# Reordering the hand-over from retention to the first expert: one weight load, one row load, the memsets and one index computation

## The chip, the cores and the metric

The kernel runs on one core of a Trainium2 chip. The metric is the device time of one execution in microseconds; the time before is the median of three runs. Two runs of this kernel differ by less than 0.2%.

## The reference, cut to what matters

```
# retention, per batch b and head h: B, H, S, D = 4, 8, 768, 64
state = gamma[h] * state + outer(k[t], v[t])
y[t]  = scale * q[t] @ state
# x: the 3072 tokens of all batches, 512 features each (8 heads x 64)
logits = x @ w_gate                       # 8 experts
e      = argmax(logits);  g = softmax(logits)[e]
out[t] = g * (relu(x[t] @ w1[e]) @ w2[e]) # w1[e]: 512 x 1024, w2[e]: 1024 x 512
```

Every token goes to exactly one expert. All arithmetic is float32; the kernel gets float32 products on TensorE from three products of a high and a low part each (hi·hi, lo·hi, hi·lo).

## The kernel before, in words

**Retention (L498 to L581).** The 24 chunks of 128 tokens are handled two at a time, in 12 passes `k` of one loop. A pass makes the scores of both chunks (`scores`, L253: TensorE L259, masked on VectorE L262), carries the state in (`carry`, L280: TensorE L289), multiplies the scores with the values (`output`, L293: TensorE L300) and turns the result into `xT` on VectorE (`turn_out`, L303, L308). It also makes the logits of the two chunks of the pass before (`logits` L328, `rows` L312, `finish_logits` L335). The order on every engine is the order in which the code is written (`manual_schedule`).

**Gating and sending.** The chunks fall into six groups (L55). For each group `choose`, `soft`, `rank`, `slots`, `weights` and `advance` (L360 to L433) find the expert of each token, its slot in that expert's region of a DRAM buffer `xs_dram`, its weight (L429) and its token number (L430), and `send_x` (L319) scatters the chunk's rows there with one indirect DMA, whose descriptors GpSimd makes (L719, about 1 us each). Behind the counted rows of an expert 96 rows are set to zero (`clear`, L325, and `clear_rows`, L713), so that a padded load reads zeros.

**Weights.** Each expert has four quarters of 1 MB (`fetch`, L135: parts 0 and 1 are w1, 2 and 3 are w2). SyncE issues these loads; they go into two buffers `raw` in turn. `split` (L142) makes the high part on ScalarE (L147) and the low part on VectorE (L148). So a quarter can be loaded only when the quarter two before it has been split in full. Expert 0's 16 split pieces lie in the passes of the loop (table `SPLITS`, L59): pieces 10 and 11, the last two of w2's first half, in pass 10. `fetch(1, 0)` (L639) therefore waits for piece 11.

**The hand-over (L583 to L679).** Expert 0 has two sets of rows. The first 192 (`xg0`, region 8) are loaded in pass 9 and computed from pass 11 on (`early_half`, L747: TensorE L761 and L779), which fills TensorE while the last groups are gated and sent. The others, `xg1`, up to 224 late rows of region 8's neighbour `E`, come only after the last chunk has been sent. SyncE's order there is: `fetch(1, 0)`, the clearing of expert 1's tail (L640), `xg1` (L641), expert 1's rows `xgs[:, 1]` (L642), three small loads of token numbers and weights into `meta0` (L643 to L645), `fetch(1, 1)` (L646), then 12 register loads (L637, L638). VectorE turns `xg1` (L729), ScalarE rounds it to the high part (L738), VectorE makes the low part (L739), and `token_index` (L194, L199 to L207) makes the scatter indices of all late rows from `meta0` (L679).

**The experts (`moe_main`, L793).** For each expert 8 blocks `f` of the first layer (TensorE L947, into PSUM tiles `phs` in turn, three of them) and then `steps` products of the second layer (L989 for experts 0 and 7, L991 for the others). After each block ScalarE makes the high part `hh` (L959) and VectorE the low part `hl` (L961). What else an engine does is put behind a block by the table `jobs` (L912): splits of the next expert's weights, loads, scatters. For expert 0 the order on VectorE behind the blocks is: `hl` of each, the splits of quarter (1, 0) behind blocks 2 and 3, of (1, 1) behind 5 and 6. Then, at the second layer, four turns of expert 1's rows (L729; three of their low parts are made by GpSimd, L739), two splits of (1, 2), and the weighted result rows (`put_rows`, L876, VectorE L882) of the two products.

**Two details.** The third product of expert 0's second layer (rows beyond 192, rarely any) stands under a branch on TensorE, with nothing on the other side (L996):

```
if e == 0 and k == 2:
    with tc.If(fewer[0] > 0):
        second_layer(cap)
```

And `moe_main` begins with four memsets of PSUM tiles on VectorE (`rare` L815, the three `phs` from column 392 on, L817) and one of `zero` on GpSimd (L825), which the scheduler puts in between the hand-over's instructions. Expert 1 and the later ones write only the columns that their token count needs (`by_count`, L834: 392 of 440 for expert 1 here), while ScalarE and VectorE read all 440. The framework orders all accesses to a bank of PSUM within a tile, whichever columns they touch.

Of the kernel before, what the change touches and what calls it, by code (L numbers as in the profile page):

```python
# [9 lines left out]
F32 = mybir.dt.float32  # L10
# [45 lines left out]
CHOSEN = {3: 0, 6: 1, 9: 2, 10: 3, 11: 4}  # L56

SENDS = {4: (0, 1), 5: (1, 3), 6: (3, 5), 7: (5, 7), 8: (7, 10), 9: (10, 12), 10: (12, 16), 11: (16, 20)}
SPLITS = {4: (0, 1), 5: (2, 3), 7: (4, 5), 8: (6, 7), 9: (8, 9), 10: (10, 11)}  # L59
FETCHES = {1: 0, 4: 1, 6: 2, 9: 3}  # L60


# [50 lines left out]
def retention_moe(ctx, tc, qkv, wts, cst, gdec, out):  # L113
# [95 lines left out]
    with ExitStack() as actx:  # L209
# [102 lines left out]
        def rows(g):  # L312
            xp = ps_s.tile([P, DM], F32, name="xp", tag="sp")
            for p in range(NP):
                nc.tensor.transpose(out=xp[:, p * P:(p + 1) * P], identity=ident,
                                    in_=xTs[g // 2][:, p, (g % 2) * C:(g % 2 + 1) * C])
            nc.scalar.copy(out=xn(g)[:, :, 0:C], in_=xp.rearrange("a (q m) -> a q m", q=4))
# [10 lines left out]
        def logits(t):  # L328
            L = ps_m.tile([P, TW], F32, name="L", tag="mm")
            for p in range(NP):  # L330
                nc.tensor.matmul(out=L[32 * p:32 * p + 32, :], lhsT=wgs[:, p, :], rhs=xTs[t][:, p, :],
                                 start=True, stop=True)
            nc.scalar.copy(out=LT, in_=L)

        def finish_logits(t):  # L335
            k = max(i for i, (a, n) in enumerate(GROUPS) if a <= 2 * t)
            first, n = GROUPS[k]
            late = int(first >= NCH // 2)
            lp = ps_m.tile([P, 2, NP, 32], F32, name="lp", tag="mm")
            for ci in range(2):  # L340
                nc.tensor.transpose(out=lp[:, ci].rearrange("t p e -> t (p e)"),  # L341
                                    in_=LT[:, ci * C:(ci + 1) * C], identity=ident)
            at = 2 * t - first
            if at == 0:
                lgs[k] = gsm.tile([P, CPB, E], F32, name="lg", bufs=2)[:, 0:n]
            nc.vector.tensor_reduce(out=lgs[k][:, at:at + 2, :], axis=AX.X, op=ALU.add,
                                    in_=lp[:, :, :, late:late + E].rearrange("t c p e -> t c e p"))

        def gating(k):
# [73 lines left out]
            def weights():  # L423
                gw = sm("gw")
                nc.vector.tensor_reduce(out=gw, in_=v["ex"], axis=AX.X, op=ALU.add)
                nc.vector.tensor_scalar(out=gw, in0=gw, scalar1=1e-9, scalar2=None, op0=ALU.add)
                a = first % (2 * CPB)
                rows = ring[:, a:a + n]
                nc.vector.reciprocal(out=rows[:, :, :, C + 1], in_=gw.broadcast_to([P, n, 4]))  # L429
                nc.vector.scalar_tensor_tensor(  # L430
                    out=rows[:, :, :, C].bitcast(I32), scalar=4.0, op0=ALU.mult, op1=ALU.add,
                    in0=k_("tok")[:, gn].unsqueeze(2).broadcast_to([P, n, 4]),
                    in1=k_("row").unsqueeze(1).broadcast_to([P, n, 4]))  # L433

            return dict(choose=choose, soft=soft, rank=rank, slots=slots, advance=advance, weights=weights)

        def fill(n):
            for i in range(state["half"], state["half"] + n):
# [145 lines left out]
        stages["rank"](ps_s, "sp")  # L584
        for name in ("slots", "weights", "advance"):
            stages[name]()
        logits(NCH // 2 - 1)
        rows(NCH - 2)
        rows(NCH - 1)
        finish_logits(NCH // 2 - 1)  # L590
        for g in range(SENDS[NCH // 2 - 1][1], GROUPS[-1][0]):
            send_x(g)
# [1 line left out]
        final["choose"]()  # L594
        final["soft"]()
        fill(FILL[1])
        lows(1, nc.gpsimd)
        final["rank"](ps_s, "sp")
        fill(FILL[2])
        final["slots"]()  # L600
# [36 lines left out]
        number = lambda i: nc.sync.value_load(eid7[0:1, i - 1:i], min_val=1, max_val=E - 1)  # L637
        end_of = lambda t, i: nc.sync.value_load(t[0:1, i - 1:i], min_val=0, max_val=(E9 + 1) * N)  # L638
        fetch(1, 0)  # L639
        clear_rows(tc, x_rows[bass.ds(end_of(end1, 1), ZROWS), :], zeros, "x_rows")  # L640
        load_x(xg1, E, NJ8)  # L641
        load_x(xgs[:, 1], 1, -(-CAPS[1] // 32))  # L642
        load_meta(meta0[EARLY - P:, 1:2], E, 1, 0, BESIDE)  # L643
        load_meta(meta0[:, 2:3], E, 1, BESIDE)
        load_meta(meta0[0:32, 3:4], E, 1, BESIDE + P, 32)  # L645
        fetch(1, 1)  # L646
        for i in range(2, E):
            expert_at[i] = number(i)
            end_at[i] = end_of(end7, i)
# [21 lines left out]
        pieces = ((0, P), (4, LATE - P))  # L671
        for j, w in pieces:
            turn_slices(nc, xt1, xg1, j, w)
        for j, w in pieces:
            cut_slices(nc, nc.vector, xhl1[:, 0], xhl1[:, 1], xt1, j, w)
        result(0, 0)
        result(0, 1)
        send(0)
        token_index(sidx0[:, 1:4], meta0[:, 1:4], lim[:, 1:4], "joint")  # L679

    def overflow():
        nc.vector.tensor_tensor(out=se, in0=sel.rearrange("p a e -> p e a"), in1=s7(k_("caps")), op=ALU.mult)
# [11 lines left out]
    def clear_behind(e, zero):  # L694
        nc.sync.dma_start(out=x_rows[bass.ds(end_at[e], ZROWS), :], in_=zero)

    natural = {0: (sidx0, meta0)}
    moe_main(tc, wparts, fetch, split, xhl1, hidden_early, third, xgs, clear_behind, load_x, load_meta, token_index, regions, beyond, limit, spare, natural,
             overflow, out)
    most = nc.values_load(top[0:1, 0:1], min_val=0, max_val=N)  # L700
    with tc.If(most > 0):
# [89 lines left out]


@with_exitstack  # L793
def moe_main(ctx, tc, wparts, fetch, split, xhl1, hidden_early, third, xgs, clear_behind, load_x, load_meta, token_index, regions, beyond, limit, spare, natural,
             overflow, out):
    nc = tc.nc
    pool = lambda name, bufs, **kw: ctx.enter_context(tc.tile_pool(name=name, bufs=bufs, reuse_waits="tile", **kw))
    PS = bass.MemoryType.PSUM
    xp = pool("xp", 2)
# [12 lines left out]
    pys = [ps_y.tile([P, DM], F32, name=f"py{i}") for i in range(2)]  # L812
    rare = ps_between.tile([P, 2, DM], F32, name="between")[:, 0]
    phs = [ps_h.tile([P, CMAX], F32, name=f"ph{i}") for i in range(3)]
    nc.vector.memset(rare[0:widths[0][2]], 0.0)  # L815
    for ph in phs:
        nc.vector.memset(ph[:, CAPS[1] - 3 * STEPS[1]:], 0.0)  # L817
    out_slices = out.rearrange("n (q m) -> (n q) m", q=4)
    sidx = tb.tile([P, E1, JMAX], I32, name="sidx")
    gw = tb.tile([P, E1, JMAX, 1], F32, name="gw")  # L820
# [1 line left out]
    sidx7 = tb.tile([P, 3], I32, name="sidx7")  # L822
    natural[E1] = (sidx7, meta7)
    zero = tb.tile([ZROWS, 4 * W], F32, name="zero")
    nc.gpsimd.memset(zero, 0.0)  # L825
    Zs = {}
    fewer = {}

# [73 lines left out]
    with tc.manual_schedule():  # L902
        for e in range(E):
# [7 lines left out]
            hs = []  # L911
            jobs = [[] for _ in range(KF + steps)]  # L912
            job = lambda f, fn, *a: jobs[f].append((fn, a))
            if e == 1:
                job(1, put_rows, 0, rare, 2)
                job(3, overflow)
# [49 lines left out]
            for k in range(steps):  # L966
                for j in range(nxt * k // steps, nxt * (k + 1) // steps) if e else range(nxt * (k == 0)):
                    prep_x(e + 1, j, nc.gpsimd if not e and j < 3 else nc.vector)
                if not e and k == 0:
                    for i, eng in halves:  # L970
                        split(1, 2, i, eng)
                py = rare if e == 0 and k == 2 else pys[k % 2]

                at_early = hidden_early

                def second_layer(cols):
                    n = 0
                    for f in range(KF):
                        whi, wlo = wparts[e, 2 + f // 4]
                        hh, hl = hs[f]  # L980
                        for a, x in ((whi, hh), (wlo, hh), (whi, hl)):
                            se = dict(start=(n == 0), stop=(n == 3 * KF - 1))
                            if e in natural:
                                j = order(e, k)
                                w = widths[e][j]
                                at = x[:, j * P:j * P + w]
                                if e == 0:
                                    at = at_early[x is hl][:, f, P:] if k == 0 else x[:, k * P - P:k * P - P + w]
                                nc.tensor.matmul(out=py[:w, :], lhsT=at, rhs=a[:, f % 4, :], **se)  # L989
                            else:  # L990
                                nc.tensor.matmul(out=py[:, :cols], lhsT=a[:, f % 4, k * P:(k + 1) * P],  # L991
                                                 rhs=x[:, :cols], **se)
                            n += 1

                if e == 0 and k == 2:
                    with tc.If(fewer[0] > 0):  # L996
                        second_layer(cap)
                elif e in natural:
                    second_layer(cap)
                else:  # L1000
                    by_count(e, second_layer)
                if e == 0 and k == 2:
                    pass
                elif e in natural:
                    put_rows(e, py, order(e, k))
                else:
                    turn(e, py, k)
                if more and k < 2:
                    for i, eng in halves:
                        if e and i == k:  # L1010
                            split(e + 1, 2, i, eng)
                if more and e and k == 0:
                    fetch(e + 1, 3)
                for fn, a in jobs[KF + k]:
                    fn(*a)
# [141 lines left out]
```

## Time and profile before

| | |
|---|---|
| median of 3 runs | 395.29 us (394.86 to 395.56) |
| the profiled execution | 394.7 us, its span 392.9 us |
| granted TensorE clock | 0.997 of full speed, mean |
| TensorE matmul busy | 379.1 us, 96% of the span |
| VectorE, ScalarE, GpSimd busy | 256.2, 154.7, 162.3 us |
| DMA | 80.65 MB, 205 GB/s over the span |

The span is the profiler's; 1.8 us of the execution lie around it. A row of a timeline has the start in us from the beginning of the span, the duration, the engine (PE is TensorE, DVE VectorE, ACT ScalarE, POOL GpSimd, SPq SyncE's queue), the line of the kernel, the operation, the tile written and those read, the shapes and the count of the instructions merged into the row. The brackets at its end give the time for which the engine stood idle before it, and what it was waiting for.

### The profile page before, as it was taken

The numbers are of one execution on the slowest core, as the hardware profiler recorded it, in microseconds if no ns is written. First come the engines' busy times: TensorE is split into PE (matmuls) and PEld (weight loads), VectorE is DVE, ScalarE is ACT, GpSimd is POOL, SyncE is SP. The second block draws the span as 40 slices with busy tenths as digits, with TensorE's granted clock in tenths as the row PEclk, the third lists the DMA queues.
The fourth block names the chain that finished last, engine by engine and source line by source line (L and its number), as shares of the span: only waits on it lengthen the run. The fifth ranks groups of instructions, "written<-read, shape, count | busy, mean of one in ns | idle before, by whom it ended". The sixth has DMA issues, their size and how long they took to land. (4 is left out here: it accounts for less than half of the span.)

```text
span 392.9 us, 8662 instructions
## 1 busy us (share of the span) xinstructions
PE 379.1 (96%) x3254; PEld 352.6 (90%) x3254; DVE 256.2 (65%) x560; ACT 154.7 (39%) x317; POOL 162.3 (41%) x155
## 2 busy tenths in 40 slices
PE   7999999998897999999999999999999999999994
PEld 4888888886796979999999999999999999999972
DVE  4547759797695767774785677477847857776330
ACT  2335545562452546533441353064235505423100
POOL 0323556846641042000752284338317623731652
PEclk9999999999999999999999999999999999999998
DMA  7998799998349389473569075735745783530111
GB/s 276 415 380 338 293 414 423 386 382 276 136 123 231 108 204 291 124 205 117 169 236 218 16 251 168 203 123 152 216 143 166 245 208 119 162 128 11 55 29 70
DMA packets 30190, 80.65 MB, mean 205 GB/s; under 512 B 4795, under 2 KB 18751, under 8 KB 23716
## 3 DMA queue, kind: packets, MB, share of 16 engines
q1 hardware_dynamic: 24868, 66.87, 52.7%
q0 software_dynamic: 5248, 12.69, 8.9%
q8 instruction: 58, 0.95, 1.1%
q14 instruction: 16, 0.13, 0.1%
HBM read 65.07 MB, written 15.19 MB: 204 GB/s over the span
## 5 line engine op out<-in xcount | busy, mean ns | idle before, releaser
L719 POOL DMA_INDIRECT out<-Z,sidx x82 | 93.5, 1140 | 134.6 <-DVE Z L897 108.6
L148 DVE TENSOR_TENSOR wlo<-raw,whi 128x1024 fp32r<-128x1024 f32 (+1 forms) x67 | 76.2, 1142 | 10.4 <-ACT whi L147 9.2
L147 ACT CAST whi<-raw 128x1024 fp32r<-128x1024 f32 (+1 forms) x72 | 67.5, 952 | 4.4 <-PE ph L947 3.8
L959 ACT ACTIVATE hh<-ph 128x64 fp32r<-128x64 f32 (+7 forms) x72 | 32.3, 461 | 91.9 <-PE ph L947 80.1
L991 PE MATMUL py<-hl,whi 128*128 128x392 f32 (+4 forms) x192 | 66.1, 344 | 0.0
L991 PE MATMUL py<-hh,whi 128*128 128x392 f32 (+4 forms) x192 | 66.0, 344 | 0.0
L991 PE MATMUL py<-hh,wlo 128*128 128x392 f32 (+4 forms) x192 | 66.0, 344 | 0.0
L961 DVE SCALAR_TENSOR_TENSOR hl<-ph,hh 128x64 fp32r<-128x64 f32 (+7 forms) x72 | 36.2, 516 | 36.7 <-ACT hh L959 34.4
L947 PE MATMUL ph<-xh,whi 128*128 128x392 f32 (+5 forms) x224 | 49.4, 342 | 0.9 <-PEq L996 0.9
L947 PE MATMUL ph<-xh,wlo 128*128 128x392 f32 (+5 forms) x224 | 49.0, 340 | 0.0
L947 PE MATMUL ph<-xl,whi 128*128 128x392 f32 (+5 forms) x224 | 49.0, 340 | 0.0
L947 PEld LDWEIGHTS ph<-xh,whi 128*128 128x128 f32 x224 | 40.3, 188 | 1.8 <-issue 1.6
L947 PEld LDWEIGHTS ph<-xh,wlo 128*128 128x128 f32 x224 | 40.4, 188 | 0.2
L947 PEld LDWEIGHTS ph<-xl,whi 128*128 128x128 f32 x224 | 40.2, 188 | 0.2
L738 ACT CAST xh<-xt 128x512 fp32r<-128x512 f32 (+7 forms) x27 | 14.9, 552 | 58.1 <-DVE xt L729 58.1
L991 PEld LDWEIGHTS py<-hl,whi 128*128 128x128 f32 x192 | 36.2, 188 | 0.2
L991 PEld LDWEIGHTS py<-hh,wlo 128*128 128x128 f32 x192 | 36.1, 188 | 0.2
L991 PEld LDWEIGHTS py<-hh,whi 128*128 128x128 f32 x192 | 36.1, 188 | 0.2
L248 POOL TENSOR_TENSOR vs<-qkv_t,cs 128x512 f32<-128x512 f32 x19 | 19.8, 1042 | 36.2 <-DMA qkv_t<-qkv 33.0
L262 DVE TENSOR_TENSOR Sb<-sp,xgs 128x512 f32<-128x512 f32 x48 | 30.0, 683 | 6.8 <-PE sp L259 6.1
L719 POOL DMA_INDIRECT xs_dram<-xn,KEY x24 | 25.0, 1043 | 15.4 <-PE lp L341 5.0
L278 ACT ACTIVATE ub<-U,cs 128x64 f32<-128x64 f32 x80 | 18.5, 314 | 27.5 <-PE U L273 27.0
(157 smaller groups left out, 515.3 us busy)
## 6 DMA issues: line engine op xcount, KB each, us to landing
raw<-w SPq DMA_DIRECT2D x32, 1024.0 KB
qkv_t<-qkv SPq DMA_DIRECT2D x18, 1024.0 KB
qkv_t<-qkv SPq DMA_DIRECT2D x4, 768.0 KB
xgs<-xs_dram SPq DMA_DIRECT2D x12, 211.2 KB
qkv_t<-qkv SPq DMA_DIRECT2D x4, 512.0 KB
xgs<-xs_dram SPq DMA_DIRECT2D x8, 227.5 KB
out<-Z,sidx POOLq DMA_INDIRECT x82
xs_dram<-zero SPq DMA_DIRECT2D x6, 195.0 KB
```

The source lines that it names most:

```text
L147: nc.scalar.copy(out=hi[:, h], in_=raw[:, h])
L148: engine.tensor_tensor(out=lo[:, h], in0=raw[:, h], in1=hi[:, h].bitcast(F32), op=ALU.subtract)
L248: engine.tensor_tensor(out=vs, in0=qs[g][:, 2].rearrange("a (h d) -> a h d", d=D), in1=cv[:, c, :].unsqueeze(2).broadcast_to([P, H, D]), o ...
L262: nc.vector.tensor_tensor(out=Sb[:, r], in0=sps[r], in1=M[:, r], op=ALU.mult)
L278: nc.scalar.activation(out=ubs[g % 3][:, p], in_=U[:, p], func=AF.Copy, scale=k_("ratio")[:, at:at + 1])
L719: sc = tc.nc.gpsimd.indirect_dma_start(out=out, out_offset=bass.IndirectOffsetOnAxis(ap=index, axis=0), in_=rows, in_offset=None, bounds_c ...
L738: nc.scalar.copy(out=xh[:, :, sl], in_=src)
L947: nc.tensor.matmul(out=ph[:, :w], lhsT=wparts[e, f // 4][a][:, kd, fo:fo + P], rhs=x[:, kd, :w], start=(n == 0), stop=(n == 3 * KD - 1))
L959: nc.scalar.activation(out=to, in_=of, func=AF.Relu)
L961: nc.vector.scalar_tensor_tensor(out=low, in0=of, scalar=0.0, in1=to.bitcast(F32), op0=ALU.max, op1=ALU.subtract)
L991: nc.tensor.matmul(out=py[:, :cols], lhsT=a[:, f % 4, k * P:(k + 1) * P], rhs=x[:, :cols], **se)
```

## The change

It moves split piece 11 out of pass 10 behind the loop, so that `fetch(1, 0)` comes after it. It moves the token numbers of the last group out of `weights`, the memsets into expert 0's jobs, and the index computation of the late rows from the hand-over to behind block 6. It loads `xg1`, `meta0` and quarter (1, 1) ahead of the clearing and ahead of expert 1's rows, makes one high part of `xg1` on VectorE in place of ScalarE, makes the first low part of the early half on VectorE in place of GpSimd (`lows(1, nc.gpsimd)` is dropped, `lows(2, nc.vector)` makes both), and gives the branch an `Else` with one small matmul.

```diff
-SPLITS = {4: (0, 1), 5: (2, 3), 7: (4, 5), 8: (6, 7), 9: (8, 9), 10: (10, 11)}
+SPLITS = {4: (0, 1), 5: (2, 3), 7: (4, 5), 8: (6, 7), 9: (8, 9), 10: (10,)}
...
-                rows = ring[:, a:a + n]
-                nc.vector.reciprocal(out=rows[:, :, :, C + 1], in_=gw.broadcast_to([P, n, 4]))
-                nc.vector.scalar_tensor_tensor(
-                    out=rows[:, :, :, C].bitcast(I32), scalar=4.0, op0=ALU.mult, op1=ALU.add,
-                    in0=k_("tok")[:, gn].unsqueeze(2).broadcast_to([P, n, 4]),
-                    in1=k_("row").unsqueeze(1).broadcast_to([P, n, 4]))
+                nc.vector.reciprocal(out=ring[:, a:a + n, :, C + 1], in_=gw.broadcast_to([P, n, 4]))
+                if not last:
+                    names(gn)
...
+        def names(gn):
+            a, n = gn.start % (2 * CPB), gn.stop - gn.start
+            nc.vector.scalar_tensor_tensor(
+                out=ring[:, a:a + n, :, C].bitcast(I32), scalar=4.0, op0=ALU.mult, op1=ALU.add,
+                in0=k_("tok")[:, gn].unsqueeze(2).broadcast_to([P, n, 4]),
+                in1=k_("row").unsqueeze(1).broadcast_to([P, n, 4]))
...
         for name in ("slots", "weights", "advance"):
             stages[name]()
+        split(0, 2, 3, nc.vector, 1)
         logits(NCH // 2 - 1)
         rows(NCH - 2)
         rows(NCH - 1)
+        names(slice(GROUPS[-1][0], NCH))
         finish_logits(NCH // 2 - 1)
...
         fill(FILL[1])
-        lows(1, nc.gpsimd)
         final["rank"](ps_s, "sp")
...
         fetch(1, 0)
-        clear_rows(tc, x_rows[bass.ds(end_of(end1, 1), ZROWS), :], zeros, "x_rows")
         load_x(xg1, E, NJ8)
-        load_x(xgs[:, 1], 1, -(-CAPS[1] // 32))
         load_meta(meta0[EARLY - P:, 1:2], E, 1, 0, BESIDE)
         load_meta(meta0[:, 2:3], E, 1, BESIDE)
         load_meta(meta0[0:32, 3:4], E, 1, BESIDE + P, 32)
         fetch(1, 1)
+        clear_rows(tc, x_rows[bass.ds(end_of(end1, 1), ZROWS), :], zeros, "x_rows")
+        load_x(xgs[:, 1], 1, -(-CAPS[1] // 32))
...
-        for j, w in pieces:
-            cut_slices(nc, nc.vector, xhl1[:, 0], xhl1[:, 1], xt1, j, w)
+        (j0, w0), (j1, w1) = pieces
+        nc.vector.tensor_copy(out=xhl1[:, 0, :, 32 * j1:32 * j1 + w1], in_=xt1[:, :, 32 * j1:32 * j1 + w1])
+        cut_slices(nc, nc.vector, xhl1[:, 0], xhl1[:, 1], xt1, j0, w0)
+        nc.vector.tensor_tensor(out=xhl1[:, 1, :, 32 * j1:32 * j1 + w1], in0=xt1[:, :, 32 * j1:32 * j1 + w1],
+                                in1=xhl1[:, 0, :, 32 * j1:32 * j1 + w1].bitcast(F32), op=ALU.subtract)
         result(0, 0)
         result(0, 1)
         send(0)
-        token_index(sidx0[:, 1:4], meta0[:, 1:4], lim[:, 1:4], "joint")
...
-    nc.vector.memset(rare[0:widths[0][2]], 0.0)
-    for ph in phs:
-        nc.vector.memset(ph[:, CAPS[1] - 3 * STEPS[1]:], 0.0)
...
-    nc.gpsimd.memset(zero, 0.0)
...
+            if e == 0:
+                job(2, nc.gpsimd.memset, zero, 0.0)
+                job(4, nc.vector.memset, rare[0:widths[0][2]], 0.0)
+                job(6, token_index, sidx0[:, 1:4], meta0[:, 1:4], lim[:, 1:4], "joint")
+                for ph in phs:
+                    job(KF, nc.vector.memset, ph[:, CAPS[1] - 3 * STEPS[1]:], 0.0)
...
                 if e == 0 and k == 2:
-                    with tc.If(fewer[0] > 0):
+                    with tc.If(fewer[0] > 0) as some:
                         second_layer(cap)
+                    with some.Else():
+                        nc.tensor.matmul(out=py[:widths[0][2], 0:128], lhsT=hs[0][0][:, P:P + widths[0][2]],
+                                         rhs=wparts[0, 2][0][:, 0, 0:128], start=True, stop=True)
```

`moe_main` gets `lim` as a further argument. `KF` is 8, so the job `KF` stands behind the first product of expert 0's second layer, after its `put_rows`.

## Rows read from the trace of the kernel before

**Rows 1.** The page: the span, and each engine's busy time.
```profile
span 392.9 us, 8662 instructions
PE 379.1 (96%) x3254; PEld 352.6 (90%) x3254; DVE 256.2 (65%) x560; ACT 154.7 (39%) x317; POOL 162.3 (41%) x155
```

**Rows 2.** Timeline of PE: expert 0's late rows, up to expert 1's first block.
```profile
120.78 0.71 PE L947 MATMUL ph<-xhl,whi 128*128 128x224 f32 x4 [1.00 <-ACT xhl L738]
...
126.21 0.71 PE L947 MATMUL ph<-xhl,whi 128*128 128x224 f32 x4 [1.15 <-DVE hl L961]
...
133.05 0.40 PE L989 MATMUL py<-whi,hh 128*128 128x512 f32 x1
...
145.17 0.99 PE L947 MATMUL ph<-xh,whi 128*128 128x392 f32 x4 [0.87 <-PEq L996]
```

**Rows 3.** Timeline of PE: the carry of pass 10, then that of pass 11.
```profile
83.96 1.10 PE L289 MATMUL Y<-qkv_t,ub 64*64 64x128 f32 x32
...
92.24 0.46 PE L289 MATMUL Y<-qkv_t,ub 64*64 64x128 f32 x5
...
95.22 0.85 PE L289 MATMUL Y<-qkv_t,ub 64*64 64x128 f32 x18 [0.46 <-issue]
```

**Rows 4.** Timeline of POOL: four scatters of chunks to the experts' regions.
```profile
79.17 1.27 POOL L719 DMA_INDIRECT xs_dram<-xn,KEY  x1 [0.16 <-issue]
...
93.40 0.98 POOL L719 DMA_INDIRECT xs_dram<-xn,KEY  x1 [0.30 <-issue]
...
108.08 0.99 POOL L719 DMA_INDIRECT xs_dram<-xn,KEY  x1 [0.58 <-DVE past L605]
109.39 1.01 POOL L719 DMA_INDIRECT xs_dram<-xn,KEY  x1 [0.31 <-issue]
```

**Rows 5.** Timeline of expert 7: the last of a run of scatters on POOL; ACT's next instruction.
```profile
371.09 0.97 POOL L719 DMA_INDIRECT out<-Z,sidx  x1 [0.30 <-issue]
...
372.14 0.49 ACT L959 ACTIVATE hh<-ph 128x380 fp32r<-128x380 f32 x1 [5.08 <-remote]
```

**Rows 6.** Windows: us, PE, PEld, DVE, ACT, POOL busy (x instructions), PEclk, DMA share, GB/s.
```profile
92.00:94.00 2.00, 1.36 (x19) 0.80 (x17) 0.70 (x6) 0.00 (x0) 1.57 (x2) 1.00 0.95 375
370.00:380.00 10.00, 10.00 (x46) 7.96 (x45) 2.65 (x7) 0.97 (x2) 5.44 (x6) 1.00 0.14 41
```

**Rows 7.** Timeline of SP: the issues of rows' and weights' loads.
```profile
84.93 2.29 SPq L186 DMA_DIRECT2D xn<-xs_dram  x4
...
88.08 0.36 SPq L139 DMA_DIRECT2D raw<-w  x1
110.81 0.01 SPq L714 DMA_DIRECT2D xs_dram<-xgs  x1
114.72 1.80 SPq L186 DMA_DIRECT2D xg<-xs_dram  x4
...
131.22 0.34 SPq L139 DMA_DIRECT2D raw<-w  x1
```

**Rows 8.** Timeline of DVE, from the last pass's tile to expert 0's results.
```profile
101.22 1.29 DVE L308 TENSOR_TENSOR xT<-Y,xgs 128x512 f32<-128x512 f32 x2 [1.60 <-PE Y L300]
...
104.57 0.22 DVE L346 TENSOR_REDUCE lg<-lp 128x16 f32<-128x64 f32 x1 [0.93 <-PE lp L341]
...
106.53 0.11 DVE L817 MEMSET ph<- 128x60 f32 x1 [0.43 <-ACT rx L765]
...
108.86 1.29 DVE L148 TENSOR_TENSOR wlo<-raw,whi 128x512 fp32r<-128x512 f32 x2
...
118.95 1.17 DVE L729 STREAM_TRANSPOSE xt<-xg 128x512 f32<-128x512 f32 x2 [1.24 <-DMA xg<-xs_dram]
...
125.41 0.17 DVE L205 TENSOR_SCALAR ids<-meta 128x3 int32<-128x3 int32 x1 [2.47 <-DMA meta<-xs_dram]
...
133.89 1.23 DVE L148 TENSOR_TENSOR wlo<-raw,whi 128x1024 fp32r<-128x1024 f32 x1 [1.97 <-ACT whi L147]
...
145.03 1.40 DVE L882 TENSOR_SCALAR yo<-py,meta 128x512 f32<-128x512 f32 x2
```

More of the change, by code (lines that the diff above doesn't have):

```diff
@@ L697, in retention_moe @@
     natural = {0: (sidx0, meta0)}
-    moe_main(tc, wparts, fetch, split, xhl1, hidden_early, third, xgs, clear_behind, load_x, load_meta, token_index, regions, beyond, limit, spare, natural,
+    moe_main(tc, wparts, fetch, split, xhl1, hidden_early, third, lim, xgs, clear_behind, load_x, load_meta, token_index, regions, beyond, limit, spare, natural,
              overflow, out)
@@ L793, in moe_main @@
 @with_exitstack
-def moe_main(ctx, tc, wparts, fetch, split, xhl1, hidden_early, third, xgs, clear_behind, load_x, load_meta, token_index, regions, beyond, limit, spare, natural,
+def moe_main(ctx, tc, wparts, fetch, split, xhl1, hidden_early, third, lim, xgs, clear_behind, load_x, load_meta, token_index, regions, beyond, limit, spare, natural,
              overflow, out):
     nc = tc.nc
+    sidx0, meta0 = natural[0]
     pool = lambda name, bufs, **kw: ctx.enter_context(tc.tile_pool(name=name, bufs=bufs, reuse_waits="tile", **kw))
```

## The prediction

> **What bounds the kernel now.** I read the page first: TensorE is busy for 379.1 us of a span of 392.9 [rows 1], so the time can fall only where TensorE stands, or where a run of its instructions takes longer than its work. The timeline of TensorE places these losses. From expert 1's first block at 145.17 us there is no gap until about 378 us, and nothing of the change reaches that far. Ahead of it there are three idle stretches [rows 2]: 1.00 us before expert 0's late rows, released by ScalarE's high part of them; 1.15 us before the fourth block, released by VectorE's `hl`; 0.87 us before expert 1, released by the branch. By starts the second is worth more: three blocks from 120.78 to 126.21 take 5.43 us, while the five from there to 133.05 take 6.84, 1.37 each; 5.43 − 4.11 leaves 1.3.
>
> The fourth loss is no idle time in the waits. The carry of pass 10 takes 1.10 us for 32 products; pass 11's begins at 92.24 and ends at 95.22 + 0.85 = 96.07, so 3.8 us [rows 3]: about 2.7 us are lost. Two things stand beside it: five scatters in a row on GpSimd, the last at 93.40 [rows 4], and expert 1's first quarter, issued at 88.08 [rows 7], with the DMA engines 95% busy at 375 GB/s [rows 6].
>
> **The carry stall (part A).** `fetch(1, 0)` moves behind piece 11, so the quarter leaves at about 104.5 us and not at 88.08. The scatters stay. Which of the two stalls TensorE is not shown by this row alone. The nearest other row is in expert 7: there ScalarE stands for 5.08 us and goes on at 372.14, just after the last scatter of a run ends at 371.09 + 0.97 = 372.06 [rows 5], with the DMA engines only 14% busy [rows 6]. So a run of scatters holds up another engine's start without a load beside it. I take most of the stall as the scatters', and give the change 0.4 us, nearer to that row than to a full recovery; bounds 0 and 2.7 us. What is gained moves the gating and the sends behind it too, since VectorE waits 1.60 us for TensorE at pass 11's result tile [rows 8], so it isn't eaten by the next wait.
>
> The Trainium skill, "DMA: Bandwidth & Descriptors", section "Issuing engines are not separate DMA queues", says that transfers started by SyncE and by GpSimd run on the same 16 engines and interleave. By it alone the load beside the scatters would be the stall's cause and its removal would return all of part A (rival 1); the row of expert 7, at 14%, speaks against that, and no run here shows it directly.
>
> Piece 11 itself costs VectorE 1.29 / 2 = 0.65 us; it lands in the 0.93 us for which VectorE stands before the logits at 104.57 [rows 8], where TensorE is late. Should that cover go (if A is gained in full), it delays the last group's gating by up to 0.65 us.
>
> **The late rows (part B).** Off VectorE's way to the last scatters go three memsets of 0.11 us or less, one of which waits 0.43 us for ScalarE [rows 8], and one index instruction; the scatter at 108.08 waits 0.58 us for VectorE [rows 4]. Together I take 0.45 us, and the two last scatters move up by that. `xg1` then waits for the last scatter instead of the clear (issued 110.81, `xg1` at 114.72 [rows 7]). But the scatter's own rows land late too: the load of the early rows left at 84.93, 4.5 us after the scatter before it ended (79.17 + 1.27) [rows 4, 7]; here it is 114.72 − 110.40 = 4.3 us after the last one. So the clear hides little, 0.1 us. VectorE's part of the high half runs beside ScalarE's: the turns end at 118.95 + 1.17 = 120.12 [rows 8], and TensorE starts 0.66 us later [rows 2], which I shorten by 0.25. Sum 0.8 us; bounds 0 (the quarter, now at 104.5, gets in the way) and the whole 1.0 of idle. The low part that VectorE takes over from GpSimd (192 columns, so less than the 0.65 us of a split piece of 512) lies off this way, since VectorE stands 1.24 us before the turns [rows 8]; GpSimd's memset of `zero` is put behind block 2, when GpSimd has sent the last rows [rows 4] and TensorE waits for nothing of it.
>
> **The fourth block (part C).** `token_index` waits 2.47 us for `meta0` [rows 8], and `hl` of the first blocks is queued behind it, for which TensorE waits. Behind block 6 the data has been there for many microseconds. The wait goes, 1.3 us; what is late next is `hl` of blocks 3 and 4, which stand behind splits of 1.2 us as at 133.89 [rows 8] and come only just in time by my reckoning. I take all of the 1.3; the bounds are 0.1 (one split too many stands ahead of `hl`) and 1.3.
>
> **The step into expert 1 (part D).** The `Else` gives TensorE a product of 128 columns on the other path, an estimated 0.1 us (a quarter of the 0.40 that one of 512 takes [rows 2]), and may save the 0.87 us at L996. But the memsets of `phs` now stand behind the first `put_rows`, and block 0 of expert 1 writes the third of these tiles, so TensorE must wait for the third memset. When is that? VectorE's chain is tied to TensorE: the split at 133.89 waits 1.97 us for ScalarE's high part [rows 8], whose buffer comes free when block 7 has read it. Block 7 starts at 133.05 − 1.37 = 131.68 [rows 2], and the chain reaches `put_rows` at 145.03 [rows 8], 13.35 us on. After the change the four instructions of `token_index` stand in that chain (0.17 each, 0.7 in all), then `put_rows` of the first product (1.40 / 2 = 0.7) and three memsets (0.11 each, 0.3): 15.1 us after block 7. TensorE now starts expert 1 at 145.17, 13.49 us after it [rows 2]. So it starts 1.6 us later than without the change; the idle time before it grows to about 2.5 us and is released by VectorE, not by the branch. Bounds: a gain of 0.9 (the memsets hold nothing up) and a loss of 1.9 (0.3 us for each semaphore).
>
> **SyncE and GpSimd.** The clear and expert 1's rows come after `fetch(1, 1)`. I estimate that the clear leaves 5 us behind `xg1`, at about 119.4, since the small loads and the quarter go between; it lands 3.9 us later as before (114.72 − 110.81 [rows 7]), and expert 1's rows take 1.8 us to issue as `xg1` does and some 4.2 to land (`xg1` left at 114.72 and was turned at 118.95 [rows 7, 8]): they are there at about 129. They are turned after the split at 133.89 [rows 8], so 4 us are spare. Quarter (1, 1) comes some 3 us earlier, which its splits, tied to blocks 5 and 6, can't use. The 12 register loads and the next quarter's load at 131.22 [rows 7] move a microsecond or so with the queue; that quarter is split only ahead of `put_rows` at 145.03 [rows 8]. All this at nothing.
>
> **The sum.** 0.4 + 0.8 + 1.3 − 1.6 = 0.9 us off the profiled execution's 394.7 (span 392.9 [rows 1] and 1.8 around it): 393.8. The median of the runs stands 0.6 above that execution, so 394.4.
>
> **The rivals.** *1, the carry stall goes with the quarter.* For: it is beside the stall at 95% DMA share [rows 6]. Against: expert 7's row [rows 5]. It adds 2.3 to part A: 392.1 us. *2, the memsets hold nothing up*, since TensorE writes columns 0 to 391 and they write from 392 on. Then D is +0.9 in place of −1.6: 391.9 us. Against: VectorE's reading of one half of pass 11's tile waits until TensorE is through with the other half [rows 8], so accesses to one bank seem to be ordered whatever the columns. The Trainium skill, "PSUM — Partial Sum Buffer", section "PSUM bank collisions raise a hardware error", says likewise that a different address in the same bank and quadrant still collides; by that rule rival 2 can't be, and 394.4 stays. *3, the parts cancel:* A gives nothing and B 0.4, since the scatter's landing and not the clear sets `xg1`: 395.2 us, no difference. *4, slower: the quarter runs into the last rows.* It moves 1 MB, at 375 GB/s [rows 6] 2.8 us, right before the last scatters. If it leaves 1.5 us later than I think, these rows land behind it, `xg1` leaves up to 2.2 us later than now, B turns from +0.8 to −2.2: 397.4 us at most. It decides when `xg1` is issued after 114.72 [rows 7]. Against: the quarter should be through by 107.5, and the last two scatters run at about 107.6 and 109.
>
> **How the numbers follow.** About 0.2%, 0.8 us, is what a measurement of this kernel can tell from no change: faster is under 394.5, slower over 396.1. The forecast (394.4, between 393.8 and 395.0) has a chance of 0.40, of which 0.22 lies below 394.5; rival 1 has 0.18, rival 2 0.10, rival 3 0.18, rival 4 0.14. Faster: 0.22 + 0.18 + 0.10 = 0.50; the same: 0.18 + 0.18 = 0.36; slower 0.14. The range goes from rival 2's 391.9 to 396.2, into rival 4, and leaves out its larger part and the case that rivals 1 and 2 come together.
>
> **What would show it.** The carry of pass 11: near 3.4 us by the forecast, 1.1 by rival 1. The first late-row product: idle about 0.2 in place of 1.00. The fourth block: no wait. Expert 1's first block: idle about 2.5, released by VectorE's memset; by rival 2 no idle. SyncE's `xg1`: at about 114 or earlier; after 114.72 is rival 4. The forecast is wrong if the carry is back to normal, if the memsets hold nothing up, or if a new wait stands between 104 and 121 us.

## The result, and the profile after

The changed kernel is slower. Its median over 11 runs is 397.63 us (396.49 to 399.58) against 395.56 for the kernel before beside it; the ratio is 1.0053, 95% interval 1.0032 to 1.0074, so 1.3 to 2.9 us. The forecast was 394.4. The 11 runs of the kernel before span 394.77 to 397.44 us, 0.7%: single executions differ by more than the 0.2% that its first three had shown.

The page of the changed kernel, its span and busy times, beside [rows 1]:

```profile
span 395.5 us, 8663 instructions
PE 381.0 (96%) x3255; PEld 354.5 (90%) x3255; DVE 257.0 (65%) x562; ACT 154.3 (39%) x316; POOL 163.0 (41%) x154
```

TensorE is busy 1.9 us longer with one product more. That is no added work: some products take longer. The timeline of TensorE in the changed kernel shows which (L289 is the carry as before, L957 the first layer that was L947):

```profile
84.83 1.10 PE L289 MATMUL Y<-qkv_t,ub 64*64 64x128 f32 x32
...
93.11 0.44 PE L289 MATMUL Y<-qkv_t,ub 64*64 64x128 f32 x4
...
96.07 0.87 PE L289 MATMUL Y<-qkv_t,ub 64*64 64x128 f32 x19 [0.97 <-issue]
...
121.27 0.68 PE L957 MATMUL ph<-xhl,whi 128*128 128x224 f32 x4 [0.61 <-DVE xhl L680]
...
143.27 0.22 PE L1009 MATMUL between<-whi,hh 128*32 128x128 f32 x1
145.92 1.64 PE L957 MATMUL ph<-xh,whi 128*128 128x392 f32 x4 [2.43 <-DVE ph L1028]
147.37 1.51 PE L957 MATMUL ph<-xh,wlo 128*128 128x392 f32 x4
148.67 1.06 PE L957 MATMUL ph<-xl,whi 128*128 128x392 f32 x4
149.57 0.87 PE L957 MATMUL ph<-xh,whi 128*128 128x392 f32 x4
```

Four things answer to [rows 2, 3]. The carry of pass 11 takes 96.94 − 93.11 = 3.83 us, as before. Before the late rows 0.61 us are idle in place of 1.00. The wait before the fourth block is gone. Before expert 1 stand 2.43 us, and the releaser is no longer the branch but a memset (L1028). Behind it is what the prediction did not forecast: the first block of expert 1 takes 149.57 − 145.92 = 3.65 us, where it took 2.25 (145.17 to 147.42) before. The windows of the changed kernel around it (columns as in [rows 6]):

```profile
140.00:146.00 6.00, 3.57 (x17) 2.66 (x15) 4.89 (x10) 2.90 (x4) 2.12 (x3) 0.97 0.69 180
146.00:150.00 4.00, 4.00 (x15) 4.00 (x16) 0.37 (x1) 0.23 (x1) 1.77 (x2) 0.62 1.17 241
150.00:154.00 4.00, 4.00 (x24) 4.00 (x23) 3.31 (x5) 2.72 (x4) 0.00 (x0) 1.00 0.67 270
```

The granted clock is 0.62 on average from 146 to 150 us: TensorE runs for most of it at the lower of its two levels, 1.2 GHz in place of 2.4, and does 15 products where the next 4 us hold 24. It had stood idle for 2.43 us just before.

VectorE's timeline of the changed kernel shows where the memset stands, beside the last of [rows 8]:

```profile
142.50 2.36 DVE L148 TENSOR_TENSOR wlo<-raw,whi 128x1024 fp32r<-128x1024 f32 x2
144.78 0.74 DVE L886 TENSOR_SCALAR yo<-py,meta 128x512 f32<-128x512 f32 x1
145.54 0.24 DVE L1028 MEMSET ph<- 128x60 f32 x3
```

Where the time went, in stages of TensorE's own work, each from the start of one row to the start of another. "Carry" is the start of pass 10's, "late" the first product of the late rows, "e1" expert 1's first block, "third" its third, "last" the start of the last product. All but the first two rows are of the experiments below, which ran in four sets.

| us | carry to late | late to e1 | e1 to third | third to last |
|---|---|---|---|---|
| before | 36.82 | 24.39 | 4.38 | 237.12 |
| changed | 36.44 | 24.65 | 5.78 | 237.19 |
| changed, second set (a1) | 36.39 | 24.69 | 5.90 | 237.08 |
| changed, fourth set (e14) | 37.69 | 24.66 | 5.88 | 237.85 |
| early memsets (e9) | 36.96 | 22.06 | 4.32 | 237.34 |
| early memsets, quarter back (e10) | 37.69 | 22.02 | 4.31 | 237.17 |

The first two profiles of the changed kernel give −0.4, +0.3, +1.4 to +1.5 and 0: 1.35 us together. The spans differ by 2.6; the other 1.25 lie ahead of pass 10 (84.83 against 83.96) and behind the last product, where the change has no part, and the profile of the second set has neither. The third gives +0.9, +0.3, +1.5 and +0.7. The second and third stage together cost the same each time, 1.7 to 1.8 us; the first and the last vary from one execution to the next.

### The profile page after: what moved, and what is told of

Read it like the earlier page. It is cut to its first block, busy times and chain, and to the rows that moved or that the text cites. A ratio compares the mean times of both kernels' runs of the same rounds, so it can differ in the third digit from the quotient of the medians.

```text
span 395.5 us, 8663 instructions
## 1 busy us (share of the span) xinstructions
PE 381.0 (96%) x3255; PEld 354.5 (90%) x3255; DVE 257.0 (65%) x562; ACT 154.3 (39%) x316; POOL 163.0 (41%) x154
## 5 line engine op out<-in xcount | busy, mean ns | idle before, releaser
L957 PE MATMUL ph<-xh,whi 128*128 128x392 f32 (+5 forms) x224 | 50.0, 345 | 2.4 <-DVE ph L1028 2.4
L957 PE MATMUL ph<-xh,wlo 128*128 128x392 f32 (+5 forms) x224 | 49.7, 344 | 0.0
L957 PE MATMUL ph<-xl,whi 128*128 128x392 f32 (+5 forms) x224 | 49.2, 341 | 0.0
L957 PEld LDWEIGHTS ph<-xh,whi 128*128 128x128 f32 x224 | 40.7, 191 | 3.1 <-issue 2.7
L957 PEld LDWEIGHTS ph<-xh,wlo 128*128 128x128 f32 x224 | 41.0, 191 | 0.2
L957 PEld LDWEIGHTS ph<-xl,whi 128*128 128x128 f32 x224 | 40.6, 190 | 0.2
```

The lines of the kernel that those rows point to most:

```text
L957: nc.tensor.matmul(out=ph[:, :w], lhsT=wparts[e, f // 4][a][:, kd, fo:fo + P], rhs=x[:, kd, :w], start=(n == 0), stop=(n == 3 * KD - 1))
```

## The experiments

The kernels of one set (the expectations say "call") ran on one chip, beside the kernel before, and only those are compared by time; across sets, ratios to before are. Before took 390.50 us on the first set's chip, 395.23, 395.18 and 395.38 on the others. A pair of numbers in brackets behind a ratio is its 95% interval. Line numbers shift by a few between kernels.

**What the memsets cost.** e1 puts each behind the block that last reads its tile:

```diff
-                for ph in phs:
-                    job(KF, nc.vector.memset, ph[:, CAPS[1] - 3 * STEPS[1]:], 0.0)
+                for f, ph in enumerate(phs):
+                    job(f, nc.vector.memset, ph[:, CAPS[1] - 3 * STEPS[1]:], 0.0)
```

> The changed kernel with the three memsets of phs behind blocks 0, 1 and 2 of expert 0 instead of behind its second layer's first product. Theory (the wait of 2.43 us for the memset in front of expert 1's first block, and the 1.4 us that its first block loses at the lower granted clock behind it, make the change slower): the wait goes to under 0.3 us, the clock stays at full speed between 146 and 150 us, 2.3 + 1.4 come off the changed kernel's 397.6: 393.9 us. Rival (the loss comes from ahead of 145 us, from the quarter now loaded between the last scatters, or from work on VectorE): 396 to 397.6 us, with the wait gone but something else in its place.

The ratio to before is 0.9964 (0.9937 to 0.9991): 1.4 us faster. No wait stands before expert 1, and no lower clock behind it. The same kernel in the third set (e9):

> The kernel with the early memsets once more, beside the one with the quarter back. Theory: no wait before expert 1's first block and no lower clock behind it, whether or not pass 11's carry stalls here: 0.996 of before. If the carry stalls on this chip (3.8 us), a wait of about 0.5 us for the late rows stays; if it does not (1.1 us), one of about 1.2 us.

The ratio is 0.9978 (0.9956 to 1.0000), a smaller gain than the expected 0.996. By the table's fifth row it takes 22.06 us from late rows to expert 1, 2.3 less than before and 2.6 less than the changed kernel, and the third block comes 4.3 us on. TensorE's rows and the window that the changed kernel has at 0.62:

```profile
122.92 0.68 PE L957 MATMUL ph<-xhl,whi 128*128 128x224 f32 x4 [0.51 <-DVE xhl L680]
...
144.98 0.93 PE L957 MATMUL ph<-xh,whi 128*128 128x392 f32 x4
...
149.30 0.88 PE L957 MATMUL ph<-xh,whi 128*128 128x392 f32 x4
```

```profile
146.00:150.00 4.00, 4.00 (x24) 4.00 (x23) 3.59 (x5) 1.92 (x4) 1.97 (x2) 1.00 1.25 212
```

Moving three memsets of 0.1 us turns the change from slower than before to faster. The wait for the late rows was 0.51 us with the carry stalled and 1.21 in the first set, as expected.

e2 is the reverse: the kernel before, with only the memsets moved to where the change has them.

> The kernel before with nothing but the three memsets moved behind the second layer's first product. Theory: VectorE gets to them about 1.0 us after 145.03, so TensorE waits about 1.9 us instead of 0.87 (1.0 more); if the granted clock falls behind a wait of that length too, 1.4 more: 398.0 us against 395.6 of before, and if it does not, 396.6. Rival (the memsets are harmless, the loss is elsewhere): 395.6 us or less.

The ratio is 1.0027 (1.0005 to 1.0049), 1.05 us slower. Its row, on TensorE:

```profile
141.18 0.94 PE L948 MATMUL ph<-xh,whi 128*128 128x392 f32 x4 [1.91 <-DVE ph L1016]
```

The wait is the expected 1.9 us, and the clock stayed at full speed behind it in the execution that was profiled: the first block took 2.20 us. Three of e2's 12 runs have a mean granted clock of 0.991 to 0.992 and the other nine 0.996 to 0.999, so in those three it was low somewhere; where is not recorded.

**What takes the clock down.** e5 puts ten products of 512 columns into the `Else`, so that TensorE works where it would wait:

```diff
                     with some.Else():
-                        nc.tensor.matmul(out=py[:widths[0][2], 0:128], lhsT=hs[0][0][:, P:P + widths[0][2]],
-                                         rhs=wparts[0, 2][0][:, 0, 0:128], start=True, stop=True)
+                        for _ in range(10):
+                            nc.tensor.matmul(out=py[:widths[0][2], :], lhsT=hs[0][0][:, P:P + widths[0][2]],
+                                             rhs=wparts[0, 2][0][:, 0, :], start=True, stop=True)
```

> The changed kernel with ten products of 512 columns in the Else in place of one of 128: some 2.3 us of TensorE work whose result nobody uses, in the place of the wait for the memset. The wait is as long as it was, but TensorE is at work in it. Theory that part of the loss is the lower clock that follows the idle wait: the first block of expert 1 takes 2.2 us instead of 3.65, 397.6 - 1.4 = 396.2 us. Rival (the slow first block comes from its operands or from the DMA traffic at that time): 397.6 us, the first block as slow as before.

The ratio is 1.0086 (1.0054 to 1.0117), 3.4 us slower than before and not the 0.6 expected, though the first block took 2.21 us. It belongs to the first set, where the profile of e2 shows no fall of the clock either, so it doesn't tell what takes the clock down. The same kernel ran again (e13) with the changed kernel beside it (e14).

> The changed kernel with ten idle-filling products in the Else once more, now beside the changed kernel. Theory (the clock falls because TensorE stands idle ahead of expert 1): the ten products take up the wait, the granted clock stays at 1.00 from 144 to 150 us and expert 1's first two blocks take 4.4 us together, where the changed kernel beside it shows 0.5 and 5.8 to 5.9; some 1.4 us faster than the changed kernel, though expert 1 starts as late. Rival (the clock falls there for another reason, the DMA traffic or the stall of pass 11): the same fall in both.

> The changed kernel itself beside the one with the filled wait. Theory: a wait of 2.4 us before expert 1, then the first two blocks in 5.8 us at a granted clock of 0.5. If pass 11's carry takes 1.1 us here and the clock does not fall behind the wait, the fall too belongs to the kind of chip on which the carry stalls.

The ratios are 1.0055 (1.0029 to 1.0080) for e13 and 1.0052 (1.0022 to 1.0082) for e14. Windows from 144 to 150 us, first of the filled kernel (e13), then of the changed one (e14):

```profile
144.00:146.00 2.00, 2.00 (x10) 0.77 (x8) 1.99 (x5) 0.00 (x0) 0.00 (x0) 1.00 0.68 148
146.00:148.00 2.00, 1.89 (x11) 1.71 (x11) 0.77 (x4) 0.00 (x0) 1.49 (x2) 1.00 1.09 241
148.00:150.00 2.00, 2.00 (x13) 2.00 (x13) 0.62 (x1) 1.27 (x2) 0.47 (x1) 1.00 1.22 232
```

```profile
144.00:146.00 2.00, 0.19 (x1) 0.23 (x2) 1.99 (x6) 0.00 (x0) 0.31 (x1) 1.00 1.13 219
146.00:148.00 2.00, 2.00 (x9) 2.00 (x9) 0.25 (x1) 0.00 (x0) 1.64 (x2) 0.69 1.24 199
148.00:150.00 2.00, 2.00 (x7) 2.00 (x7) 0.14 (x1) 0.71 (x2) 0.00 (x0) 0.50 1.11 309
```

With work in the wait the clock stays at 1.00 and the first two blocks take 4.34 us; with idleness it falls to 0.50 and they take 5.88. The carry of pass 11 stalled in both (4.11 and 4.24 us), so the stall isn't what parts them. Nor is the DMA traffic: here are the four microseconds from expert 1's first product on, in e13, e14, e2 and e11 (the last is below):

```profile
146.32:150.32 4.00, 4.00 (x23) 4.00 (x24) 1.16 (x3) 1.47 (x2) 1.84 (x2) 1.00 1.18 255
145.81:149.81 4.00, 4.00 (x15) 4.00 (x16) 0.44 (x1) 0.52 (x2) 1.83 (x2) 0.62 1.19 243
141.18:145.18 4.00, 4.00 (x23) 4.00 (x24) 1.16 (x3) 1.47 (x2) 1.84 (x2) 1.00 1.22 226
146.33:150.33 4.00, 4.00 (x14) 4.00 (x15) 1.11 (x2) 0.03 (x1) 1.97 (x2) 0.57 1.24 195
```

The DMA share is 1.18 to 1.24 in all four, and the clock fell in the one with the least throughput and not in the one with the most. So the rival is out: here the idle time takes the clock down. All runs bear it out: the granted clock, averaged over the 12 runs, is 0.9910 in e14, 0.9942 in e13 and 0.9933 in the kernel before, and 0.9904 against 0.9939 in the second set's changed kernel and before. Of some 396 us these differences are 0.9 to 1.4 us.

My time for e13 was wrong all the same, since it lost elsewhere what it won here. Two later rows of its timeline carry most of it: a wait for a result row on VectorE (1.37 us), and one at the start of a later expert (1.09 us), which stood in e5 too (0.87 us). Why the `Else` of ten brings the second is open.

```profile
210.29 0.46 PE L1001 MATMUL py<-hh,whi 128*128 128x422 f32 x1 [1.37 <-DVE Z L896]
...
329.11 0.93 PE L957 MATMUL ph<-xh,whi 128*128 128x366 f32 x4 [1.09 <-issue]
```

The changed kernel itself, in the second set (a1):

> The changed kernel itself, unaltered, beside the ones of this call and for comparison with the runs in which pass 11's carry took its normal 1.10 us. Theory that the wait for the memsets is the loss whatever the carry does: 2.4 us idle before expert 1's first block, and, if the lower clock belongs to that wait, the first block at 3.6 us instead of 2.2 again; 1.005 times the time of before, 2 us more. Rival (it was the carry stall of that one profile that brought the clock down): the wait is there, the first block takes 2.2 us, about 0.5 us more than before.

The ratio is 1.0071 (1.0044 to 1.0099); the wait is 2.45 us and the fall is there, as the table shows. The carry stalled here as well (3.86 us), so a1 by itself doesn't part the wait from the stall; e9 and e13 do, which have the stall and no fall at expert 1. e11 moves the memsets in front of the first `put_rows`:

> The changed kernel with the three memsets in front of the first product's put_rows instead of behind it: they end some 0.7 us earlier, so TensorE waits about 1.7 us in place of 2.43. It tells from which length of the wait on the clock falls here. If the clock falls behind this wait too: expert 1's first two blocks together take 1.4 us longer than 4.4, 0.7 us less than the changed kernel. If not: 2.1 us less than the changed kernel, about the time of before.

The ratio is 1.0036 (1.0009 to 1.0063). The wait is 1.78 us, and the clock falls behind it too; the first block takes 3.77 us, 1.5 too long:

```profile
146.33 1.54 PE L955 MATMUL ph<-xh,whi 128*128 128x392 f32 x4 [1.78 <-DVE ph L1018]
...
150.10 0.88 PE L955 MATMUL ph<-xh,whi 128*128 128x392 f32 x4
```

So in the profiles there was no fall behind 0.87 us, there was one behind 1.78 and 2.4, and none behind 1.91 in e2. The length alone doesn't decide: the changed kernel itself has a run with a mean clock of 0.998 in a1 and one of 0.997 in e14, as high as in the profiles without a fall (0.997 in before, e1 and e2).

**The index computation.** e3 is the kernel before with only `token_index` moved behind block 6.

> The kernel before with nothing but the late rows' index computation moved behind block 6. Theory by the prediction's part C: the wait of 1.1 to 1.2 us before the fourth block goes and nothing takes its place there; VectorE's chain to the result rows grows by 0.7 us, which nothing waits for here, since the memsets are where they were: 1.2 to 1.3 us less than before. Rival (the wait moves to the fifth or the seventh block, behind the splits): the same time as before.

The ratio is 0.9965 (0.9935 to 0.9994), 1.4 us faster. The wait before the fourth block is gone, the next blocks wait for nothing, and the branch's wait is as it was:

```profile
121.78 0.71 PE L949 MATMUL ph<-xhl,whi 128*128 128x224 f32 x4 [0.16 <-ACT xhl L737]
144.74 0.97 PE L949 MATMUL ph<-xh,whi 128*128 128x392 f32 x4 [0.87 <-PEq L998]
```

From late rows to expert 1 it takes 22.96 us in place of 24.39. e9 has 0.9 less again: that is the size of the branch's wait, which is gone there. The `Else` was not tried alone.

**The quarter and the carry.** e8 is the kernel before with only piece 11, and so `fetch(1, 0)`, moved:

```diff
-SPLITS = {..., 10: (10, 11)}
+SPLITS = {..., 10: (10,)}
...
             stages[name]()
+        split(0, 2, 3, nc.vector, 1)
         logits(NCH // 2 - 1)
```

> The kernel before with nothing but piece 11 moved behind the loop, and so the first quarter of expert 1 behind it. Theory: 0.7 to 1.4 us slower than before, the late rows' load about 1 us later against pass 10's carry. Rival (the move takes a load away from the carry and the scatters): faster by up to 2.7 us.

The ratio is 1.0006 (0.9977 to 1.0034): no difference clear of the noise, where I had expected 0.7 to 1.4 us more. The carry of pass 11 takes 95.60 + 0.91 − 92.58 = 3.93 us without the quarter beside it, which left at 105.23. e7 and e10 put piece 11 back into pass 10 and keep the early memsets and the rest of the change.

> The kernel with the early memsets and piece 11 back in pass 10, so that expert 1's first quarter is loaded at about 88 us again; all else as in the change. Theory (where the carry takes its normal time, piece 11 stands on VectorE's way to the last gating, 0.7 us, and the quarter at 101 us makes the last rows land later): the late rows' load leaves about 1 us earlier against pass 10's carry, TensorE's waits between 100 and 121 us fall from 2.2 to about 1.0, 0.997 of before becomes 0.994. Rival (the quarter beside the five scatters is what stalls the carry, where it stalls): the carry takes 3.8 us, and 2 us come back.

> Early memsets and quarter (1, 0) at 88 us once more. Theory (the quarter's place has nothing to do with the carry, and its move puts 0.7 us of piece 11 on the way to the last rows): the carry as in the run beside it, TensorE's wait for the late rows under 0.3 us, 0.5 to 1 us faster than the run beside it. Rival (the carry stalls with the quarter beside it and not without): slower than the run beside it.

The ratios are 0.9961 (0.9932 to 0.9990) for e7, where I had expected 0.994, and 0.9932 (0.9908 to 0.9955) for e10, beside e9's 0.9978. TensorE doesn't wait for the late rows in either. The carry takes 3.91 us in e10, as without the quarter. In the first set it took 1.10 with the quarter (e2) and without (e1, e5). So rival 1 is out in both directions: whether the carry stalls depends on the chip or the set, not on the quarter. e10 is the fastest kernel here, 2.7 us under before. Why it beats e9 by nearly 2 us in the medians is not in the profiles: the table has 0.5 us of wait gone, and 0.7 us more from carry to late, with a lower clock at 104 to 108 us that e9 has at 98 to 102. Part of it is the clock of the other runs: 0.9944 on average in e10 and 0.9929 in e9, some 0.6 us.

**The scatters and the carry.** e6 (early memsets) and e12 (e10's kernel) send one chunk later, so that four scatters follow each other beside the carry in place of five:

```diff
-SENDS = {..., 10: (12, 16), 11: (16, 20)}
+SENDS = {..., 10: (12, 15), 11: (15, 20)}
```

> The kernel with the early memsets, and one scatter fewer in the run beside pass 11's carry: chunk 15 is sent in pass 11 instead of pass 10 (table SENDS), so four scatters follow each other without a pause instead of five. Theory (the run of scatters holds TensorE up, not the quarter, since the stall of 2.7 us is there in the changed kernel without it): the carry of pass 11 ends 1.3 us earlier against its start, 393.9 - 1.3 = 392.6 us. Rival (the stall has another cause, or the wait only moves): 393.9 us, the carry at 3.8 us as before.

> Early memsets, quarter at 88 us, and one scatter fewer in the run beside pass 11's carry (chunk 15 sent in pass 11). Only where the carry stalls does this tell: if the run of scatters stalls it, the carry ends 1.3 us earlier against its start and 0.5 to 1.3 us come off; if not, the carry takes as long as in the runs beside it. Where the carry takes 1.1 us anyway, a scatter more behind it delays GpSimd's low part of the early rows: 0.3 us or more slower.

e6 ran where the carry doesn't stall, so it is no test; its ratio is 1.0014 (0.9981 to 1.0046), above e1's 0.9964. e12 is one. First e10's rows of TensorE and GpSimd, then e12's:

```profile
92.50 0.46 PE L289 MATMUL Y<-qkv_t,ub 64*64 64x128 f32 x3
...
93.67 0.97 POOL L725 DMA_INDIRECT xs_dram<-xn,KEY  x1 [0.31 <-issue]
...
95.50 0.91 PE L289 MATMUL Y<-qkv_t,ub 64*64 64x128 f32 x20 [0.44 <-issue]
...
103.48 0.64 PE L331 MATMUL L<-xT,xgs 128*32 128x256 f32 x8 [1.77 <-DVE rk L391]
```

```profile
91.82 0.97 POOL L725 DMA_INDIRECT xs_dram<-xn,KEY  x1 [0.30 <-issue]
...
91.93 0.44 PE L289 MATMUL Y<-qkv_t,ub 64*64 64x128 f32 x3
...
93.48 1.03 PE L289 MATMUL Y<-qkv_t,ub 64*64 64x128 f32 x26 [0.28 <-issue]
...
102.91 0.68 PE L331 MATMUL L<-xT,xgs 128*32 128x256 f32 x8 [3.10 <-DVE rk L391]
```

The run of scatters ends at 94.64 in e10 and at 92.79 in e12, and the carry 1.8 and 1.7 us behind it: 3.91 us and 2.58. The stall follows the scatters. But the scatter put off joins the next run, and the wait before the logits grows from 1.77 to 3.10, which takes back the 1.33 us exactly. By time e12 is at 1.0008 (0.9989 to 1.0027): the expected gain of 0.5 to 1.3 us didn't come, and it is 2.6 us behind e10, more than its profile shows. About 1 us of that is the clock, 0.9917 on average against 0.9944.

## Why the prediction was wrong

**The step that failed** is part D, by a term that it did not have. "So it starts 1.6 us later than without the change; the idle time before it grows to about 2.5 us and is released by VectorE" came out nearly to the digit: 2.43 us, released by the memset, 1.56 more than 0.87. But the sum went on as if TensorE came out of that wait at full speed. The lower clock behind it costs 1.4 to 1.5 us more (table, third column; e13 against e14), so D is −3.0 and not −1.6. Its bound for a loss, 1.9, held the wait alone and was too small; of the 0.3 us that it allows for a semaphore, 0.14 are there, from the memsets' end (145.54 + 0.24) to TensorE's start at 145.92. With 1.4 off the forecast's gain of 0.9, the sum is a loss of 0.5; with the 0.4 each that parts A and B lack (below), 1.3, which is what the profiles show. The range ended at 396.2, and 1.4 us less would have put the median of 397.63 on that end. None of the three signs that the prediction gave for being wrong came.

**Part A** was taken as 0.4 and is nothing: 3.83 us against 3.8, and e8 shows it alone. The reason was right, since the stall follows the scatters (e12). The rule of the Trainium skill by which rival 1 would hold ("DMA: Bandwidth & Descriptors", "Issuing engines are not separate DMA queues") decides nothing here: the carry stalls alike with the quarter (3.91 us, e10) and without (3.93 us, e8).

**Part B** was taken as 0.8 and measures 0.4 (idle time 0.61 for 1.00, 36.44 us for 36.82). Three terms were wrong and partly make up for each other. The last scatter did not move up by 0.45; against pass 10's carry it ran 0.7 us later (111.00 − 84.83 = 26.17 for 25.43), and why is open, since e7 has 26.0 with piece 11 back in pass 10. The clear hid more than 0.1: without it `xg1` leaves 114.94 − 112.17 = 2.8 us behind the end of the last scatter, not 4.3. And VectorE's part of the high half saved nothing: the turns end at 120.63 and TensorE starts 0.64 us later, for 0.66 before, where 0.25 were to come off.

```profile
111.00 1.17 POOL L726 DMA_INDIRECT xs_dram<-xn,KEY  x1 [0.30 <-ACT hh L773]
119.46 1.17 DVE L736 STREAM_TRANSPOSE xt<-xg 128x512 f32<-128x512 f32 x2 [0.84 <-DMA xg<-xs_dram]
```

```profile
105.20 0.36 SPq L139 DMA_DIRECT2D raw<-w  x1
114.94 2.06 SPq L186 DMA_DIRECT2D xg<-xs_dram  x4
...
120.58 0.36 SPq L721 DMA_DIRECT2D xs_dram<-xgs  x1
124.76 1.99 SPq L186 DMA_DIRECT2D xgs<-xs_dram  x4
```

So the early rows' load, 4.5 us behind its scatter, was no measure of how late a scatter's rows land. Rival 4 did not come, though the median lies near its 397.4: `xg1` left at 114.94, but 0.65 us earlier than before against the carry. SyncE's order held as worked out, and expert 1's rows were there in time.

**Part C** was right: the wait is gone, 1.4 us by e3's stage and 1.4 by its median.

**Rival 2** is out: the memsets hold TensorE up though they write other columns. The sentence of the Trainium skill on a different address in one bank ("PSUM — Partial Sum Buffer", "PSUM bank collisions raise a hardware error") fits the 2.43 us, but the wait shows how the framework orders, not what the hardware would do without it; no run here shows that.

What stays open: some 0.3 to 0.8 us of the median's 2.1, and 1.0 to 1.5 of the 2.8 in the second set. A lower clock somewhere between 96 and 108 us, as in e14 (0.50 from 96 to 98 us), would make it up, but e3, e8, e9 and e10 have one too, so it is no part of the change alone. Nor is before free of it: in the three sets in which the carry stalls, 53 of its 89 runs have a mean clock under 0.995, and in the first set one of 31. Its profile, at 0.997, shows one of the runs without.

## What to carry to other kernels

Price a wait on TensorE with what follows it: here 1.6 us more of idleness cost 3.0 in the profiles, because the next products ran at half the clock. An instruction of 0.1 us moved "out of the way" is as late as the queue that it is put into, so ask who writes the tile next; behind its tile's last reader it cost nothing. A change of many parts is best tried part by part: the index computation and, it seems, the `Else` gained 2.3 us between the late rows and expert 1, and three memsets hid all of it.

## What the runs showed of the hardware that I had not expected

The granted clock fell to its lower level behind an idle time of 1.78 us at expert 1 (e11), and stayed down for 3 to 4 us of full work. It needs no single gap of that length: in e9 it fell right behind the stalled carry (0.57 on average from 98 to 102 us), in which no gap was longer than 0.96 us.

Beside a run of scatters on GpSimd, TensorE's carry came to its last unbroken row of products only 0.7 to 0.9 us after the run's end (before, e10, e12), and ended 1.7 to 2.1 us after it in the profiles of before, of the changed kernel and of sets two to four. In the first set it didn't stall at all, though e2's program is the same up to there; before took about 5 us less in that set. What differs was not found.
